# More passes of a zero tile in TensorE's planned gaps of the first stage, and a last store in two parts

## The chip, the core and the metric

One core of a Trainium2 chip runs the whole program. Its engines are TensorE (PE in the rows, with its weight loads as PEld), VectorE (DVE), ScalarE (ACT), GpSimd (POOL) and SyncE (SP, which issues all DMAs here). Each takes its instructions strictly in order, and they wait for each other by semaphores. The metric is the device time of one execution in microseconds (us).

## The reference

Causal attention over 4 x 12 heads of 448 x 64, then two feed-forward layers over 1792 tokens of 768 numbers:

```python
scores = scale * np.matmul(q, k.transpose(0, 1, 3, 2))     # causal mask, softmax
x = np.matmul(attn, v)                                     # -> (1792, 768)
h = (x @ w1) * (x @ w2) @ w3
x = h @ w_out                                              # d_ff 1024
h = x @ w_in                                               # d_ff 2048
out = (h - np.tanh(h)) @ w_out2
```

## The kernel before

The product w3 times w_out does not depend on the tokens. The kernel forms it first, as sixteen tiles of 128 x 384, and weaves this with the attention of the first two batches: that is the first stage, up to about 150 us. Numbers are split in a high and a low part, so that each product is three matmuls on fp32r operands (L598 to L600: high times low, low times high, high times high); the products of the attention run on plain float32.

For one pair of heads the attention goes round the engines: scores on TensorE (L683), masking and row maximum on VectorE (L646), exponentials on ScalarE (L696), 20 transposes of the probabilities on TensorE (L720), their copies `pt` out of PSUM on ScalarE (L341), probabilities times values on TensorE (L749) with four transposes of the reciprocal sums (L759), a copy `xp` on ScalarE (L763) and its scaling on VectorE (L765). ScalarE, VectorE and GpSimd also convert the weights that arrive by DMA (`raw`, L382 to L399; high part L341, low part L344).

The order of all instructions is set when the program is built, by a planner (`Plan`). Each piece of work is a flow that asks for an engine and a time; `run` picks what can start first, by planned times. Where TensorE's next instruction would by plan start more than `GAP` after the end of the one before it, `run` calls `plan.idle` with the planned gap. That function (in `start`) issues a number of passes of `none`, a 128 x 128 tile of zeros, into columns 384 and up of the second PSUM tile, which hold zeros and which nobody reads. The planner books no time for these passes. `plan.idle` is set for the first stage alone. Thirteen such passes (`WARM`) stand ahead of all other work of TensorE.

In the last stage (`Second.lowered`) each product of the last layer is added into an accumulator on VectorE (L1382) and, in the last quarter, stored by SP (L1389). The last product is quarter 3, pair 2, i = 6 of the second half. Behind the last store SP comes to the end of the program: a branch on a flag (L1798), which skips a second body that computes the same without an approximation, and the closing barriers.

Of the kernel before, what the change touches and what calls it, by code (L numbers as in the profile page):

```python
# [23 lines left out]
ALU = mybir.AluOpType  # L24

B, H, S, D = 4, 12, 448, 64
NT, DM, FF, FF2 = 1792, 768, 1024, 2048
P = 128
# [102 lines left out]
class Plan:  # L131


    LAG, DMA_LAG, MARGIN = 0.12, 2.0, 0.5
    FILLER, GAP = 1000, 1.0

    def __init__(self):
        self.free = dict.fromkeys(("PE", "ACT", "DVE", "POOL", "DMA"), 0.0)
# [116 lines left out]
def act(n, psum=False):  # L255
    return "ACT", (0.104 if psum else 0.147) + n / 1400
# [3 lines left out]
def dve(n):  # L260

    return "DVE", 0.068 + n / 960
# [25 lines left out]
def dma(size):  # L288
    return "DMA", max(0.5, size / 330e3)
# [3 lines left out]
def body(ctx: ExitStack, tc: tile.TileContext, qkd, vd, vd4, w12, w3t, wo, w_in, wo2, out, flag=None):  # L293
    nc = tc.nc
    V, A, G, SP, PE = nc.vector, nc.scalar, nc.gpsimd, nc.sync, nc.tensor
# [44 lines left out]
    def copy(eng, out, in_):  # L340
        A.copy(out=out, in_=in_) if eng == "ACT" else V.tensor_copy(out=out, in_=in_)  # L341
# [810 lines left out]
    class Second:  # L1152
# [218 lines left out]
        def lowered(self, q, pair, i, buf, seen):  # L1371

            out_ = {0: (0, 0), 1: (0, 0), 2: (0, 1), 3: (1, 1), 4: (1, 1), 5: (0, 1), 6: (1, 0)}[i]
            m, t = 2 * pair + out_[0], out_[1]
            a = self.acc[pair].t[:, out_[0], t * S:(t + 1) * S]
            if i in (1, 4, 5):
                yield seen[{1: 0, 4: 3, 5: 2}[i]]
            if q == 0 and i in (0, 2, 3, 6):
                copy((yield [act(S, True), dve(S)]), a, buf.t[:, :S])
            else:  # L1380
                yield dve(S)
                V.tensor_tensor(out=a, in0=buf.t[:, :S], in1=a, op=ALU.add)  # L1382
            plan.set(seen[i])
            if i in (1, 5, 6):
                plan.done(buf)
            if q == 3 and i in (1, 4, 5, 6):
                yield dma(P * S * 4)
                d = self.half * W + t * S
                SP.dma_start(out=out[m, :, d:d + S], in_=a)  # L1389
                self.left[pair] -= 1  # L1390
                if self.left[pair] == 0:
                    plan.done(self.acc[pair])
# [41 lines left out]
    def first_half(r_asb, r_raw, r_t, r_u, x):  # L1434
        yield from product(r_asb, r_raw, r_t, jobs_12, jobs_in + jobs_out, [wps[m] for m in WP] + w12s + twos)
        plan.spawn(sums(pairs_in, r_u), 500)
        plan.spawn(sums_out(pairs_out, r_u), 500)
        ab = []
        for _ in range(2):
            ab.append((yield r_g))  # L1440
        yield from bilinear(jobs_12, x.t, x_ready[:2], r_asb, ab, ab_ready[0])
        plan.done(x)
        plan.set(l1_over)
        tile = project(wps, ab, ab_ready[0], 0, lambda m: r_st[0], opened)
        for m in WP:
            yield from tile(m, range(8), there_and_back())
        for a in ab:
            plan.done(a)
        plan.set(l2_over)

    def start(r_asb, r_raw, r_t, r_u, at, aps):
        none = at.tile([P, P], F32R, name="none")
        V.memset(none.bitcast(F32), 0.0)
        V.memset(r_mm.tiles[1][:, 384:], 0.0)

        def idle(gap):

            for _ in range(int(0.7 * (gap - 0.5) / 0.107)):
                PE.matmul(r_mm.tiles[1][:, 384:], none, none, start=False, stop=False, skip_group_check=True)

        plan.idle = idle
        for _ in range(WARM):
            PE.matmul(r_mm.tiles[1][:, 384:], none, none, start=False, stop=False, skip_group_check=True)
        x = yield r_x
        xa["over"] = attention(at, aps, x.t)
        plan.spawn(first_half(r_asb, r_raw, r_t, r_u, x), plan.FILLER)
        plan.set(spawned)
# [336 lines left out]
```

## Time and profile before

| | us |
|---|---|
| median of three runs (lowest, highest) | 1010.18 (1008.81, 1011.15) |
| profiled execution, its own time | 1009.07 |
| span of its trace | 1007.3 |
| TensorE busy | 987.6 |
| VectorE busy | 796.1 |
| ScalarE busy | 624.7 |

A row of the time line gives the start, the duration, the engine and line, what is written and read, and how many instructions run together; in brackets the idle time of the engine before it and what ended that. A matmul's duration reaches to its modelled end and overlaps the next one, so the spacing of starts tells the rate. A plain float32 product of L683 or L749 has two rows in the trace. The granted clock (PEclk) is given as a share of 2.4 GHz; 0.50 is the level of 1.2 GHz.

### The profile page before, as it was taken

The page shows a single profiled execution, that of the slowest core. Times are in us where ns is not written, and L with a number is a line of the kernel's source. Part 1 is how long each engine was busy: PE and PEld are TensorE (multiplying, and loading weights), DVE is VectorE, ACT ScalarE, POOL GpSimd, SP SyncE. Part 2 cuts the span into 40 slices and gives each one's busy share as a digit, 9 for nine tenths or more (in the row PEclk, how much of TensorE's full clock was granted, in tenths as well). Part 3 has the DMA queues.
Part 4 walks back from the last instruction along what each step waited for, and adds up shares of the span by engine and source line. Part 5 has one row for each costly group of instructions (what it writes and reads, how often), then busy time and mean ns, then how long its engine had stood idle before and what let it go on. Part 6 is the DMA issues. An engine that isn't in the chain of part 4 may idle for free.

```text
span 1007.3 us, 20299 instructions
## 1 busy us (share of the span) xinstructions
PE 987.6 (98%) x7437; PEld 867.9 (86%) x7437; DVE 796.1 (79%) x1759; ACT 624.7 (62%) x1482; POOL 94.6 (9%) x76
## 2 busy tenths in 40 slices
PE   9889999999999999999999999999999999999997
PEld 6668678888888889899889899999999999999996
DVE  6778885777778657888887388897999896869894
ACT  7997775877778624444445456886676656645540
POOL 2443201122232110000000000000000000000000
PEclk9999999999999999999999999999999999999999
DMA  7566648767786789899999878978689786666443
GB/s 239 190 207 203 216 135 272 266 204 251 249 312 214 247 312 331 292 322 318 320 337 366 320 266 294 320 260 263 228 292 312 213 254 201 182 191 182 146 136 114
DMA packets 119021, 251.25 MB, mean 249 GB/s; under 512 B 11072, under 2 KB 70464, under 8 KB 118144
## 3 DMA queue, kind: packets, MB, share of 16 engines
q1 hardware_dynamic: 118912, 249.87, 73.9%
q8 instruction: 60, 0.98, 0.4%
q14 instruction: 49, 0.40, 0.1%
HBM read 170.20 MB, written 79.63 MB: 248 GB/s over the span
## 4 chain that ended last, share of the span: by engine, by line
PE 86%; ACT 5%; DVE 4%; DMA 3%; issue 1%; POOL 0%; SPq 0%; DVEq 0%; ACTq 0%
PE mm L598 13%; PE mm L600 12%; PE mm L599 12%; PE mm L1363 7%; PE mm L1188 7%; PE mm L1187 7%; PE mm L1365 7%; PE mm L1189 7%; PE mm L1364 7%; PE pv L904 3%; PE sc L884 3%; DMA raw<-w3t 1%; ACT p L696 1%; DMA raw<-wo 1%; PE att L749 1%; ACT pt L341 1%
## 5 line engine op out<-in xcount | busy, mean ns | idle before, releaser
L598 PE MATMUL mm<-x,hl 128*128 128x384 f32 (+1 forms) x384 | 141.9, 369 | 0.0
L600 PE MATMUL mm<-x,hl 128*128 128x384 f32 (+1 forms) x384 | 139.5, 363 | 0.0
L599 PE MATMUL mm<-x,hl 128*128 128x384 f32 (+1 forms) x384 | 139.4, 363 | 0.0
L1188 PE MATMUL mm<-x,hl 128*128 128x448 f32 x336 | 122.8, 365 | 0.0
L1189 PE MATMUL mm<-x,hl 128*128 128x448 f32 x336 | 122.7, 365 | 0.0
L1187 PE MATMUL mm<-x,hl 128*128 128x448 f32 x336 | 122.7, 365 | 0.0
L1382 DVE TENSOR_TENSOR acc<-mm,acc 128x448 f32<-128x448 f32 x144 | 89.2, 620 | 21.8 <-PE mm L1365 21.1
L598 PE MATMUL mm<-g,hl 128*128 128x384 f32 (+1 forms) x272 | 98.5, 362 | 2.4 <-POOL g L344 2.4
L382 ACT ACTIVATE raw<-raw 128x512 uint32<-128x512 uint32 (+1 forms) x80 | 64.1, 802 | 56.9 <-DMA raw<-w 17.2
L599 PE MATMUL mm<-g,hl 128*128 128x384 f32 (+1 forms) x272 | 95.2, 350 | 0.9 <-POOL hl L344 0.9
L600 PE MATMUL mm<-g,hl 128*128 128x384 f32 (+1 forms) x272 | 95.2, 350 | 0.0
L598 PEld LDWEIGHTS mm<-x,hl 128*128 128x128 f32 x384 | 72.0, 188 | 10.8 <-issue 2.5
L600 PEld LDWEIGHTS mm<-x,hl 128*128 128x128 f32 x384 | 72.1, 188 | 7.7
L599 PEld LDWEIGHTS mm<-x,hl 128*128 128x128 f32 x384 | 72.1, 188 | 7.4
L399 DVE CUSTOM_DVE_ANT_0 t<-raw,t 128x1024 uint16<-128x1024 uint16 (+1 forms) x80 | 69.5, 868 | 4.8 <-ACT raw L382 0.5
L395 DVE SCALAR_TENSOR_TENSOR t<-raw,t 128x512 uint32<-128x512 uint32 (+1 forms) x80 | 70.5, 881 | 1.2
L1187 PEld LDWEIGHTS mm<-x,hl 128*128 128x128 f32 x336 | 63.1, 188 | 5.2
L1188 PEld LDWEIGHTS mm<-x,hl 128*128 128x128 f32 x336 | 63.1, 188 | 5.1
L1189 PEld LDWEIGHTS mm<-x,hl 128*128 128x128 f32 x336 | 63.1, 188 | 4.9
L344 POOL TENSOR_TENSOR hl<-t,hl 128x512 fp32r<-128x512 f32 (+1 forms) x32 | 51.1, 1598 | 173.7 <-ACT hl L341 130.2
L341 ACT CAST x<-x 128x256 fp32r<-128x256 f32 (+2 forms) x83 | 39.7, 495 | 36.2 <-DMA x<-scx 17.7
L392 DVE TENSOR_SCALAR t<-raw 128x512 uint32<-128x512 uint32 (+1 forms) x80 | 44.0, 550 | 22.3 <-POOL hl L344 6.9
(190 smaller groups left out, 2346.0 us busy)
## 6 DMA issues: line engine op xcount, KB each, us to landing
scs<-hl SPq DMA_DIRECT2D x56, 384.0 KB, 4.3
hl<-scs SPq DMA_DIRECT2D x56, 384.0 KB, 3.3
raw<-w SPq DMA_DIRECT2D x16, 768.0 KB, 6.1
raw<-w_in SPq DMA_DIRECT2D x16, 768.0 KB, 6.2
raw<-wo SPq DMA_DIRECT2D x24, 512.0 KB, 5.7
sco<-cvo SPq DMA_DIRECT2D x24, 512.0 KB, 5.6
qk<-qkd SPq DMA_DIRECT2D x24, 448.0 KB, 3.9
v<-vd SPq DMA_DIRECT2D x12, 896.0 KB, 7.4
```

Source lines behind the costliest of these rows:

```text
L395: V.scalar_tensor_tensor(out=t, in0=raw[:, :n, 1], scalar=0xC0000000, in1=t, op0=ALU.bitwise_and, op1=ALU.bitwise_or)
L399: V.tensor_tensor(out=t, in0=t, in1=raw[:, :n, 0], op=ALU.add)
L598: PE.matmul(ps, wh, xl, start=k == 0, stop=False)
L599: PE.matmul(ps, wl, xh, start=False, stop=False)
L600: PE.matmul(ps, wh, xh, start=False, stop=k == last)
L1187: PE.matmul(ps, wh, xl, start=first and k == 0, stop=False, skip_group_check=True)
L1188: PE.matmul(ps, wl, xh, start=False, stop=False, skip_group_check=True)
L1189: PE.matmul(ps, wh, xh, start=False, stop=k == KH - 1, skip_group_check=True)
L1363: PE.matmul(ps, wh, xl, start=first and k == 0, stop=False, skip_group_check=True)
L1364: PE.matmul(ps, wl, xh, start=False, stop=False, skip_group_check=True)
L1365: PE.matmul(ps, wh, xh, start=False, stop=k == 1, skip_group_check=True)
L1382: V.tensor_tensor(out=a, in0=buf.t[:, :S], in1=a, op=ALU.add)
```

## The change

Two numbers and a formula of the planner, and one store. `GAP` goes from 1.0 to 0.6, so passes are also put into shorter planned gaps. Their number was 0.7 times the gap less 0.5, over 0.107; it becomes the gap less 0.25, over 0.107. In all there are 108 passes in place of 54. In `lowered` the addition and the store of the last product are cut into two halves of 224 columns.

```diff
-    FILLER, GAP = 1000, 1.0
+    FILLER, GAP = 1000, 0.6
...
+            cuts = [(0, S)]
+            if (self.half, q, pair, i) == (1, 3, 2, 6):
+                cuts = [(0, S // 2), (S // 2, S)]
             if q == 0 and i in (0, 2, 3, 6):
                 copy((yield [act(S, True), dve(S)]), a, buf.t[:, :S])
             else:
-                yield dve(S)
-                V.tensor_tensor(out=a, in0=buf.t[:, :S], in1=a, op=ALU.add)
+                for o, e in cuts:
+                    yield dve(e - o)
+                    V.tensor_tensor(out=a[:, o:e], in0=buf.t[:, o:e], in1=a[:, o:e], op=ALU.add)
...
-                yield dma(P * S * 4)
                 d = self.half * W + t * S
-                SP.dma_start(out=out[m, :, d:d + S], in_=a)
+                for o, e in cuts:
+                    yield dma(P * (e - o) * 4)
+                    SP.dma_start(out=out[m, :, d + o:d + e], in_=a[:, o:e])
...
         def idle(gap):
-            for _ in range(int(0.7 * (gap - 0.5) / 0.107)):
+            for _ in range(int((gap - 0.25) / 0.107)):
                 PE.matmul(r_mm.tiles[1][:, 384:], none, none, start=False, stop=False, skip_group_check=True)
```

The order of the other instructions stays as it was on every engine; only passes are added on TensorE. By place, in the order of time, the groups go from 16, 13, 0, 4, 3, 13, 0, 0, 5, 0 passes to 26, 21, 3, 9, 7, 21, 3, 3, 10, 5. Three of the places follow; `none` is the zero tile, `qk` queries and keys, `p` the probabilities, `g` and `hl` the parts of w_out and w3.

TensorE at the start, the first two pairs of heads:

```order
 L683 MATMUL att<-qk 112x224 x2
 L683 MATMUL att<-qk 112x112 x2
-L1459 MATMUL mm_82<-none 128x128 x16
+L1464 MATMUL mm_82<-none 128x128 x26
 L683 MATMUL att<-qk 112x336 x2
 L683 MATMUL att<-qk 112x224 x2
 L683 MATMUL att<-qk 112x112 x2
-L1459 MATMUL mm_82<-none 128x128 x13
+L1464 MATMUL mm_82<-none 128x128 x21
 L720 MATMUL att<-ident,p 112x112 x20
+L1464 MATMUL mm_82<-none 128x128 x3
 L683 MATMUL att<-qk 112x448 x2
```

Ten passes more stand ahead of the second pair's scores, eight more ahead of the first transposes, and three behind those.

TensorE at about 30 us of the trace before, ahead of a product of w3 and w_out:

```order
 L683 MATMUL att<-qk 112x224 x2
 L683 MATMUL att<-qk 112x112 x2
-L1459 MATMUL mm_82<-none 128x128 x4
+L1464 MATMUL mm_82<-none 128x128 x9
 L598 MATMUL mm_81<-g,hl 128x384
 L599 MATMUL mm_81<-g,hl 128x384
 L600 MATMUL mm_81<-g,hl 128x384
```

Five passes more stand between the scores and the product.

TensorE at about 38 us, within the transposes of the third pair:

```order
 L600 MATMUL mm_82<-g,hl 128x384
 L720 MATMUL att<-ident,p 112x112 x8
-L1459 MATMUL mm_82<-none 128x128 x3
+L1464 MATMUL mm_82<-none 128x128 x7
 L720 MATMUL att<-ident,p 112x112 x12
 L598 MATMUL mm_81<-g,hl 128x384
```

Four passes more part the first eight transposes from the other twelve.

## Rows read from the trace of the kernel before

**Rows 1.** Page, part 1: busy us (share of the span) xinstructions.

```profile
PE 987.6 (98%) x7437; PEld 867.9 (86%) x7437; DVE 796.1 (79%) x1759; ACT 624.7 (62%) x1482; POOL 94.6 (9%) x76
```

**Rows 2.** Chain of waits in order of time, 9 to 60: start us, us, what.

```profile
13.88 3.18 ACT p L696 x12
...
17.06 2.02 ACT pt L341 x3
```

**Rows 3.** Time line, TensorE, 29 to 45.

```profile
29.61 0.66 PE L1459 MATMUL mm<-none 128*128 128x128 f32 x4
32.04 0.44 PE L598 MATMUL mm<-g,hl 128*128 128x384 f32 x1 [1.77 <-POOL g L344]
...
32.76 3.41 PE L749 MATMUL att<-pt,v 112*64 112x448 f32 x16
36.09 0.93 PE L759 MATMUL att<-ident,rr 112*128 112x112 f32 x4
...
38.10 0.53 PE L1459 MATMUL mm<-none 128*128 128x128 f32 x3
38.47 1.33 PE L720 MATMUL att<-ident,p 112*112 112x112 f32 x12
...
42.29 2.11 PE L749 MATMUL att<-pt,v 112*64 112x448 f32 x16
44.33 0.60 PE L759 MATMUL att<-ident,rr 112*128 112x112 f32 x4
```

**Rows 4.** Time line, ScalarE, 30 to 48.

```profile
37.06 0.53 ACT L763 COPY xp<-att 128x448 f32<-128x448 f32 x1 [1.47 <-PE att L759]
...
39.13 2.14 ACT L341 COPY pt<-att 112x896 f32<-112x896 f32 x3
```

**Rows 5.** Stretches: us, busy us of PE, PEld, DVE, ACT, POOL; PEclk, DMA, GB/s.

```profile
9.51:33.40 23.89, 20.65 (x160) 15.57 (x160) 21.85 (x67) 23.34 (x64) 7.91 (x5) 1.00 0.64 215
33.40:36.81 3.41, 3.41 (x19) 1.94 (x15) 2.44 (x6) 2.19 (x8) 1.14 (x1) 0.50 0.53 193
36.82:1002.70 965.88, 955.22 (x7234) 844.65 (x7232) 769.05 (x1676) 596.26 (x1408) 83.87 (x57) 1.00 0.75 251
```

**Rows 6.** The end: time line, SP's waits (total, times, longest), last store's landing.

```profile
1000.02 0.62 DVE L1382 TENSOR_TENSOR acc<-mm,acc 128x448 f32<-128x448 f32 x1 [0.59 <-PE mm L1365]
...
1000.68 0.33 SPq L1389 DMA_DIRECT2D out<-acc  x1
...
SPq L1798 <- SPq L1798: 3.0, 1, 3.0
...
DMA to landing us min/median/max: 2.8/2.8/2.8
```

**Rows 7.** Time line, TensorE and its weight loads (PEld), 0 to 19.

```profile
1.24 3.04 PE L1463 MATMUL mm<-none 128*128 128x128 f32 x13 [1.24 <-DVE mm L1454]
...
9.66 2.00 PE L1459 MATMUL mm<-none 128*128 128x128 f32 x16
...
11.59 1.67 PE L683 MATMUL att<-qk 64*112 64x336 f32 x12
...
14.70 1.82 PE L720 MATMUL att<-ident,p 112*112 112x112 f32 x14
...
15.34 0.95 PEld L720 LDWEIGHTS att<-ident,p 112*112 112x112 f32 x10 [0.30 <-ACT p L696]
...
17.41 0.79 PE L720 MATMUL att<-ident,p 112*112 112x112 f32 x6 [0.89 <-DVE st L646]
...
18.13 2.15 PE L683 MATMUL att<-qk 64*112 64x448 f32 x16
```

**Rows 8.** TensorE's waits, 0 to 130: us in total, times, longest us.

```profile
PE att L720 <- DVE p L660: 1.6, 1, 1.6
...
PE att L683 <- DVE xp L765: 1.1, 1, 1.1
```

**Rows 9.** Time line, VectorE: masking and maximum of 224 columns.

```profile
9.78 0.39 DVE L646 CUSTOM_DVE_ANT_0 p<-att,mask 112x224 f32<-112x224 f32 x1 [1.04 <-PE att L683]
```

## The prediction

> **What bounds the kernel now.** I read the page first: TensorE is busy 98% of the span [rows 1], so on the whole the kernel is as long as TensorE's work. Nearly all of that lies outside the change; the edits touch the first 72 us and the last 7 us. So I read those two pieces.
>
> In the first stage (attention woven with w3 times w_out) the chain of waits does not run over TensorE. From 11 to 30 us nearly all of it is ScalarE: exponentials, then the copies pt that empty the transposes, and at its end GpSimd's subtraction [rows 2]. What TensorE does later there costs time only where ScalarE, or that subtraction, is late for it. From 32 to 37 us the chain is on TensorE: after an idle 1.77 us that GpSimd ends, three products of w3 and the L749 products run, and ScalarE waits 1.47 us for L759 [rows 3, 4]. In the stretches of the span the granted clock is 1.00 from 9.51 to 33.40, 0.50 (the 1.2 GHz level) from 33.40 to 36.81, then 1.00 again [rows 5]. The same 16 rows of L749 take 3.41 us there and 2.11 us at 42.29; the four of L759 take 0.93 and 0.60 [rows 3]. So the one low-clock stretch of the stage follows its longest idle time, and it stands where TensorE is waited for.
>
> At the end, the last addition of VectorE runs 0.62 us from 1000.02, the last store is issued at 1000.68, and it lands 2.8 us later, at 1003.5. But SP has a wait of its own of 3.0 us there, in the branch at L1798, right behind the issue [rows 6]; the issue ends at 1001.01, so the branch holds SP until about 1004. The landing lies within it.
>
> **The change part by part.**
>
> *The price of a pass.* The 16 passes from 9.66 take 2.00 us [rows 7], of which the last one is about 0.28: (2.00 - 0.28)/15, 0.115 us each. The planner books no time for them, so nothing else moves in the order; whatever they last beyond the real gap is delay of the next real instruction.
>
> *First three groups, 16 to 26, 13 to 21 and a new 3.* Behind the passes of before the score products start at 11.59 and the transposes at 14.70 without idle time [rows 7]: the passes already fill the real gaps. The 10 + 8 more put the transposes back by up to 18 x 0.115 = 2.07 us. Of this 0.30 us is wait for ScalarE in mid-group, so TensorE would stand about 1.8 us late. The first eight transposes are ready at about 14.70 + 0.30 + 8 x 0.11 = 15.9 us (14 take 1.82 with that wait), and ScalarE takes them at 17.06 [rows 2, 7], which covers 1.1 to 1.2 us. So ScalarE, and with it the chain, is 0.6 us late. The later half of the transposes, at 17.41, had 0.89 us of idle and is late by what VectorE is; the 3 passes ahead of 18.13 add 0.35 to that, some 0.85 together, and the chain by then runs on ScalarE, 0.6 late. Term: +0.6. Bounds: 0 if the cover is larger than I count (TensorE's earlier instructions have slack that the waits don't show), 2.07 + 0.35 = 2.4 if nothing covers.
>
> *4 to 9 at 29.61.* Five more are 0.58 us in an idle time of 1.77 us that ends with GpSimd's result, not with TensorE [rows 3]. Covered: 0. What is late next is still that result.
>
> *3 to 7 at 38.10.* The transposes follow at 38.47 without idle, and ScalarE's copies of them start at 39.13 and run on without a gap, so the second copy soon needs them [rows 3, 4]. 4 x 0.115 = 0.46 us with little cover: +0.4, between 0 and 0.46.
>
> *The other groups.* 13 to 21 at about 45 is 8 x 0.115 = 0.92 us in the 1.1 us for which L683 waits for VectorE's xp [rows 8]. The 3, 3 and 5 new ones and the 5 to 10 at 61 are 3 or 5 passes more, 0.35 to 0.58 us each, in a stretch whose chain is ScalarE's, and TensorE meets later waits for other engines that take them up. I take 0; the upper bound is 3 + 3 + 5 + 5 passes, 1.8 us.
>
> *The clock.* With the five more passes the idle time at 30 shrinks from 1.77 us to about 1.2 (TensorE and GpSimd both come some 0.6 later there, which leaves the difference as it is). If the clock stays up, L749 and L759 take 2.11 and 0.60 us as at 42.29, in place of 3.41 and 0.93: 1.6 us less on TensorE, of which ScalarE can use the 1.47 us that it waits [rows 3, 4]. Term: -1.5, or 0 if the clock falls all the same. I take -1.5, as waits of 1.1 and even of 1.6 us (L720, for VectorE's p) later in the stage did not bring it down: from 36.82 to the end of the work it is 1.00 [rows 5, 8].
> The Trainium skill ("TensorE: Matmul & The Clock Gate", section "Why this matters for your kernels") warns only of idle gaps longer than any in this stage; by it the clock would not have fallen at 33.4 and the passes had nothing to win. Here the trace disagrees, since it fell behind an idle 1.77 us; what the rule would give is the first rival's time.
>
> *The last store.* VectorE's addition becomes two halves. No row has this addition at 224 columns; the nearest, L646, which reads the same kind of source, takes 0.39 us there [rows 9], so two halves take 0.78 in place of 0.62 and the second ends 0.16 us later. The first store's issue, 0.33 us [rows 6], ends before that. SP reaches its branch 0.16 us later, at most 0.33 (if the two issues stand in a row). A gain would need the landing to be last; it isn't, by 0.5 us. Term: +0.15, between 0 and 0.33.
>
> **The sum.** +0.6 + 0.4 - 1.5 + 0.15 = -0.35, say -0.4 us. The profiled execution took 1009.07 us (span 1007.3, 1.8 around it), 1.1 less than the median of the three runs, which range from 1008.81 to 1011.15. They differ by steps about as large as one low-clock stretch costs, so I set the sum against the mean of all four, 1009.8: **1009.4 us**.
>
> **The rivals.**
>
> *The clock falls all the same* (there, or a little later). For it: 1.2 us of idle time are left, and the passes are added work at every other place. Against: the wait of 1.6 us that left the clock alone [rows 8]. +0.6 + 0.4 + 0.15 = +1.15: 1010.9 us.
>
> *Passes ahead of the rise of the clock* (the slower side). At the start the 13 warm-up passes take 3.04 us, 3.04/13 = 0.23 us or a little less each, against 0.115 from 9.66 on [rows 7]: the clock rose only just ahead of the first group. Where it rises after it, ten more passes there cost up to 2.2 us in place of 1.15, and the 16 of before have already eaten the 1.1 us of cover: 2.2 + 8 x 0.115 - 0.30 = 2.8, with 0.4 and 0.15 it is +3.35, or +1.85 if the later fall is avoided: 1011.7 to 1013.2 us. It decides from the point where the clock rises later than about 9.7. The one trace can't say how often.
> The Trainium skill (same page, section "Part 1: The HAM clock gate") says that the point of the rise differs from run to run of one kernel, since the monitor is not started with it; by it this rival is to be reckoned with, and no run here shows it.
>
> *The delays are covered* and the clock stays up. For it: ScalarE and VectorE are busy nearly all the time from 9.51 to 33.40 [rows 5], so TensorE may have more slack than single waits show. -1.5 + 0.15: 1008.4 us; with a second low-clock stretch gone that the longer runs may have had, 1006.9.
>
> *The change does nothing*: the passes fill planned gaps, and where these aren't gaps on the chip they are only delay. That is within the first rival.
>
> **How the numbers follow.** My forecast 0.45, the fall all the same 0.25, the covered delays 0.20, the late rise 0.10. About 0.2% (2 us) is what a measurement of this kernel can tell from no change. Faster than that: the lower half of the covered case and the edge of the forecast, 0.15; slower: the late rise and the edge of the first rival, 0.12; within: 0.73. The range leaves out the late rise and the lower half of the covered case: from 1008.4 down by the spread of runs to 1007.6, and from 1010.9 up to 1011.5. The upper ends of the terms together, 2.4 + 0.46 + 1.8 + 0.33 - 1.5 = +3.5 us, would need that no cover holds anywhere; the range goes half that far.
>
> **What would show it.** Right: no stretch with a granted clock of 0.50 between 10 and 100 us; L749 at 32 to 35 us in 2.1 us; the transposes at 14.7 start 1.5 to 2 us later and ScalarE's first copy pt at 17.5; the w3 products at 32.04 at 32.6; the second half of the last addition ends 0.1 to 0.2 us later after the last product, and SP's branch still takes 3.0. Wrong: a low-clock stretch anywhere in the first 130 us, the first copy at 17.0 (covered) or beyond 18.5 (late rise or no cover), or a branch so short that the landing is last.

## The result, and the profile after

The changed kernel took 1017.93 us in the median of 7 runs (1013.43 to 1023.23), the kernel before 1008.81 (1008.56 to 1011.15). The ratio is 1.0082, with an interval of 1.0054 to 1.011: about 0.8% slower, and outside the range that I gave. The profiled execution took 1014.38 us; its span is 1012.6 against 1007.3, so 5.3 us of the loss can be read in the traces.

**The first stage shows no loss of this size.** Stretches of the span (columns as in [rows 5]):

```profile
10.00:32.00 22.00, 20.93 (x173) 17.23 (x172) 20.14 (x58) 20.21 (x52) 6.78 (x5) 1.00 0.58 198
32.00:37.00 5.00, 3.79 (x27) 2.52 (x28) 4.73 (x13) 5.00 (x16) 1.29 (x2) 1.00 0.58 174
37.00:100.00 63.00, 58.93 (x422) 47.68 (x421) 49.35 (x134) 55.25 (x144) 26.74 (x19) 1.00 0.63 210
```

The stretch at 0.50 of [rows 5] is gone. The time line of TensorE, 9 to 41 us, answers to [rows 3, 7] (L1464 are the passes):

```profile
9.48 3.12 PE L1464 MATMUL mm<-none 128*128 128x128 f32 x26
12.53 1.40 PE L683 MATMUL att<-qk 64*112 64x336 f32 x12
13.86 2.56 PE L1464 MATMUL mm<-none 128*128 128x128 f32 x21
16.25 1.52 PE L720 MATMUL att<-ident,p 112*112 112x112 f32 x14
18.68 0.79 PE L720 MATMUL att<-ident,p 112*112 112x112 f32 x6 [0.91 <-DVE st L646]
...
30.76 1.22 PE L1464 MATMUL mm<-none 128*128 128x128 f32 x9
33.21 0.44 PE L598 MATMUL mm<-g,hl 128*128 128x384 f32 x1 [1.23 <-POOL g L344]
...
33.93 2.11 PE L749 MATMUL att<-pt,v 112*64 112x448 f32 x16
35.97 0.60 PE L759 MATMUL att<-ident,rr 112*128 112x112 f32 x4
...
40.79 1.57 PE L683 MATMUL att<-qk 64*112 64x448 f32 x8
```

TensorE is 1.55 us late at the transposes (16.25 against 14.70) and 1.17 us late at the w3 product (33.21 against 32.04). L749 then takes 2.11 in place of 3.41 us, and the scores at 40.79 start at the same time in both traces. In these two traces the passes had won about what they had cost; at 341 us the changed kernel stands only 0.19 us behind (341.03 against 340.84, below).

**The loss lies at 341 to 362 us**, in the second stage, 270 us behind the last edited place ahead of it. TensorE's waits from 150 us to the end of its work; before's trace has no row there:

```profile
PE pv L904 <- issue: 3.2, 3, 2.3
```

"issue" is time in which TensorE waited for nothing that the profile shows. L904 is the product of turned probabilities and values: bursts of 96 or 104 matmuls on 32 partitions, some 14 ns each, between runs of wide matmuls (L598 to L600, about 0.2 us each). TensorE's time line, after:

```profile
341.03 0.90 PE L904 MATMUL pv<-pt,v 32*64 32x128 f32 x45
342.60 0.90 PE L904 MATMUL pv<-pt,v 32*64 32x96 f32 x51 [0.66 <-issue]
...
348.28 0.82 PE L904 MATMUL pv<-pt,v 32*64 32x64 f32 x56
349.34 0.86 PE L904 MATMUL pv<-pt,v 32*64 32x32 f32 x48 [0.24 <-issue]
...
351.72 1.21 PE L904 MATMUL pv<-pt,v 32*64 32x128 f32 x73
355.21 0.56 PE L904 MATMUL pv<-pt,v 32*64 32x96 f32 x23 [2.28 <-issue]
```

and the same three bursts before, each in one piece:

```profile
340.84 1.52 PE L904 MATMUL pv<-pt,v 32*64 32x128 f32 x96
...
347.14 1.44 PE L904 MATMUL pv<-pt,v 32*64 32x64 f32 x104
...
350.11 1.52 PE L904 MATMUL pv<-pt,v 32*64 32x128 f32 x96
```

Count the matmuls between the waits. From the first wait to the second TensorE runs 51 small, 21 wide and 56 small matmuls: 128. From the second to the third it runs 48, 6 and 73: 127. Each matmul comes with a weight load, so that is 256 instructions (other instructions, such as semaphore events, make up the odd one). The profile's queues name what comes in such pieces, before and after:

```profile
q8 instruction: 60, 0.98, 0.4%
...
q8 instruction: 61, 1.00, 0.4%
```

After, that is 61 packets of together 1.00 MB, 16 KB each, in a queue of the kind "instruction"; before it is 60. 7491 pairs of a load and a matmul, at 128 to a packet, make 58.5. So the kernel fetches TensorE's instructions in packets of 16 KB, 128 matmuls each, and all three waits stand where such a block ends. The change put 54 passes, 108 instructions, ahead of all of the second stage. Every block end of that stage so moved by 54 matmuls, from the wide matmuls behind the bursts into the bursts.

The Trainium skill ("Runtime: NRT & Kernel Launch", section "Instruction fetch mechanics") gives the size, 16 KiB and 256 instructions, and the trace agrees with its 128 pairs. It also says that the cost of passing such a boundary is mostly hidden; here it showed, with 0.24 to 2.28 us.

**The sum of the profiled execution.** Behind before, in us: 0.19 at 341.03; 4.13 behind the third wait (355.69 against 351.56 at the next wide matmul), so 3.94 for three waits with their restarts; 4.59 at the last addition (1004.61 against 1000.02), where a fourth, shorter interruption at 361 adds most of the 0.46; and 0.70 in the closing, which makes the 5.3.

The end (last additions, and SP's waits in the last ten us, answering to [rows 6]):

```profile
1004.61 0.69 DVE L1386 TENSOR_TENSOR acc<-mm,acc 128x224 f32<-128x224 f32 x2 [0.59 <-PE mm L1365]
...
SPq L1803 <- SPq L1803: 4.8, 3, 2.8
```

Two halves take 0.69 us where the whole took 0.62. The branch on the flag (now L1803) still takes 2.8, but behind it SP waits another 2 us on itself, where before's rows have 3.0 in all.

### The profile page after: what moved, and what is told of

Its sections match the earlier page's. It is cut to its first block, busy times and chain, and to the rows that moved or that the text cites. A ratio compares the mean times of both kernels' runs of the same rounds, so it can differ in the third digit from the quotient of the medians.

```text
span 1012.6 us, 20410 instructions
## 1 busy us (share of the span) xinstructions
PE 992.2 (98%) x7491; PEld 873.5 (86%) x7491; DVE 795.5 (79%) x1760; ACT 623.3 (62%) x1482; POOL 93.8 (9%) x76
## 4 chain that ended last, share of the span: by engine, by line
## 5 line engine op out<-in xcount | busy, mean ns | idle before, releaser
L598 PE MATMUL mm<-x,hl 128*128 128x384 f32 (+1 forms) x384 | 141.9, 369 | 0.0
L600 PE MATMUL mm<-x,hl 128*128 128x384 f32 (+1 forms) x384 | 139.5, 363 | 0.0
L1386 DVE TENSOR_TENSOR acc<-mm,acc 128x448 f32<-128x448 f32 (+1 forms) x145 | 88.9, 614 | 19.3 <-PE mm L1365 18.8
L598 PE MATMUL mm<-g,hl 128*128 128x384 f32 (+1 forms) x272 | 98.6, 362 | 1.9 <-POOL g L344 1.9
L600 PE MATMUL mm<-g,hl 128*128 128x384 f32 (+1 forms) x272 | 95.3, 350 | 0.0
L598 PEld LDWEIGHTS mm<-x,hl 128*128 128x128 f32 x384 | 72.0, 188 | 10.7 <-issue 2.5
L600 PEld LDWEIGHTS mm<-x,hl 128*128 128x128 f32 x384 | 72.1, 188 | 7.7
L344 POOL TENSOR_TENSOR hl<-t,hl 128x512 fp32r<-128x512 f32 (+1 forms) x32 | 51.1, 1600 | 174.7 <-ACT hl L341 130.8
L344 DVE TENSOR_TENSOR x<-x 128x256 fp32r<-128x256 f32 (+2 forms) x90 | 46.7, 530 | 22.7 <-ACT x L341 22.2
```

What stands on the lines that cost most here:

```text
L344: (V if eng == "DVE" else G).tensor_tensor(out=out, in0=in0, in1=in1, op=ALU.subtract)
L598: PE.matmul(ps, wh, xl, start=k == 0, stop=False)
L600: PE.matmul(ps, wh, xh, start=False, stop=k == last)
L1386: V.tensor_tensor(out=a[:, o:e], in0=buf.t[:, o:e], in1=a[:, o:e], op=ALU.add)
```

## The experiments

Theory: the loss is no work of the change but the place of TensorE's code. Rivals: the work of the passes, the store, or the mere length of the code.

**The passes alone, and the store alone.** The first is before with the two edits to `GAP` and the number of passes, the second before with only the last addition and store in two parts.

```diff
-    FILLER, GAP = 1000, 1.0
+    FILLER, GAP = 1000, 0.6
-            for _ in range(int(0.7 * (gap - 0.5) / 0.107)):
+            for _ in range(int((gap - 0.25) / 0.107)):
```

> The passes of the change alone, the last store in one piece as before. Theory (code): TensorE's instructions come in blocks of 16 KB by DMA; 54 passes more are 108 instructions more, so the ends of the blocks fall elsewhere in the bursts of L904, and TensorE waits there for code. Then this is like the changed kernel: 3 to 10 us above the kernel before, idle time of L904 that ends with nothing visible (issue) of 2 to 8 us. Rival (store): the loss comes with the two halves of the store, and this is within 1 us of the kernel before.

> The last store in two halves alone, passes as before. Theory (code): TensorE's instructions are those of the kernel before, so no new waits of L904; the end is 0.15 us later: 1008.8 to 1009.2 us. Rival (store): 1012 us or more.

Passes alone: 1015.06 us, ratio 1.0059 (1.0039 to 1.0078), and TensorE's waits behind 150 us are nearly those of the whole change:

```profile
PE pv L904 <- issue: 3.7, 3, 2.3
```

Store alone: 1009.48 us, ratio 1.0006 (0.9985 to 1.0027), and no such row. The passes make the loss.

**Their work, or their place in the code.** The 54 passes that the change adds are shrunk to 32 x 32, so that they do a small part of the work but are as many instructions:

```diff
+            for _ in range(int((gap - 0.25) / 0.107) - n):
+                PE.matmul(r_mm.tiles[1][:32, 384:416], none[:, :32], none[:, :32], start=False, stop=False, skip_group_check=True)
```

> The full passes of the kernel before, and each of the 54 added passes shrunk to 32 x 32: as many instructions as the changed kernel, little of the added work. Theory (code): the ends of the code blocks are where the changed kernel has them, so TensorE waits for code in L904 as there: 1012 to 1020 us, issue waits of 2 us or more in the profile. Rival (time): the loss comes from the work and the shift in time of the full passes; with a third of that work 1009 to 1010 us and no issue waits.

1016.05 us, ratio 1.0062 (1.0043 to 1.0082), "PE pv L904 <- issue" 3.3 us in three waits. The loss doesn't come from the work of the passes; their number makes it.

**More code, with the block ends back in place.** All passes of the change in full, and 74 small ones more (37 ahead of the w3 product at 32 us, 37 ahead of the first transposes of the seventh pair): 54 + 74 = 128, one whole block. Once with one last store, once with the changed kernel's two.

```diff
+            calls[0] += 1
+            for _ in range(37 if calls[0] == 4 else 0):
+                PE.matmul(r_mm.tiles[1][:32, 384:416], none[:, :32], none[:, :32], start=False, stop=False, skip_group_check=True)
...
+                if n == 6 and js == (0,):
+                    plan.small(37)
```

> The passes of the changed kernel (store in one piece) and 74 small passes of 32 x 32 more, half of them ahead of the w3 product at 32 us and half ahead of the transposes of the seventh pair at 96 us, where TensorE idles: 128 matmuls with their weight loads more than the kernel before, that is 256 instructions or one block of 16 KB at 64 bytes each. Theory (code): from 97 us on the ends of the blocks stand to the bursts of L904 as in the kernel before, and the waits for code go away: 1007.5 to 1009.5 us. Rival (time): the full passes are all there and so is the loss, 1013 us or more. Rival (more code costs more): above the changed kernel.

> The changed kernel, store in two parts and all, with 74 small passes (37 ahead of the w3 product at 32 us, 37 ahead of the first transposes of the seventh pair), so that 128 matmuls more than before's stand ahead of the later code and the block ends fall where they did. Theory: no issue wait at L904, ratio 0.998 to 1.003 to before. Rival (the store in two parts and the passes together cost what neither showed alone): ratio above 1.004 without issue waits.

One store: 1009.7 us, ratio 1.0007 (0.9989 to 1.0025). Two stores: 1009.58 us, ratio 1.0009 (0.999 to 1.0028). Neither has an issue wait, and the bursts run in one piece (time line of TensorE, the kernel with two stores):

```profile
339.60 1.52 PE L906 MATMUL pv<-pt,v 32*64 32x128 f32 x96
...
345.90 1.44 PE L906 MATMUL pv<-pt,v 32*64 32x64 f32 x104
...
348.87 1.52 PE L906 MATMUL pv<-pt,v 32*64 32x128 f32 x96
```

So the change with 148 instructions on top is as fast as before. The three rivals (work, store, length of the code) fall.

**Other places.** 27 and 91 small passes added to before.

```diff
+            for _ in range({3: 27}.get(calls[0], 0)):
...
+            for _ in range({2: 17, 3: 37}.get(calls[0], 0)):
```

> The kernel before with 27 small passes (32x32) added behind the group of 4 at 30 us: 54 more instructions, which move the ends of TensorE's code blocks 27 matmuls earlier in the work behind. Theory: the ends at 337 to 361 us fall on the 72nd of the 96 small matmuls, the 83rd of the 104, and four matmuls behind the third burst; from the stalls of the changed kernel (0.7, 0.2 and 2.3 us at the 45th, 56th and 73rd) and the time that a block takes here, issue waits of 0.5 to 1.4 us at the first, 0 to 0.3 at the second, and 0.8 to 1.2 at the third, which now stands at L598 to L600: 1.5 to 2.9 us in all, and 0.3 to 1.5 us over the kernel before if the clock stretch goes with them. Rival (only a shift of about half a block hurts, or the stalls have no place in the code): no issue wait.

> The kernel before with 91 small passes added (17 at 15 us, 37 at 31 us, 37 ahead of the first transposes of the seventh pair): block ends 91 matmuls earlier. Theory: they fall on the 8th, 19th and 36th matmul of the same three bursts; a block then holds the bursts with few wide matmuls between, its 128 matmuls run in 3.3 to 4.4 us, and the next block is there no sooner than some 5.4 to 5.9 us behind the last: issue waits of 3 to 4.5 us in all, 1.5 to 3.5 us slower than before. Rival (more instructions cost in proportion): between the result of 54 more and twice that, 7 to 9 us slower. Rival (it matters only where an end lies past the middle of a burst): under 1 us of issue waits.

With 27: 1011.25 us, ratio 1.0024 (1.0009 to 1.0038). The ends stand where they were expected, on the 72nd and the 83rd small matmul and on the fourth wide one behind the third burst, with 2.0 us of waits, within the forecast. The time is not: 2.5 us above the 1008.76 us of before's runs beside it, where 0.3 to 1.5 was expected. The stretch at 0.50 didn't go; its trace has two of them in the first stage, from 45.67 and from 96.87. The waits (time line of TensorE):

```profile
341.94 0.56 PE L904 MATMUL pv<-pt,v 32*64 32x96 f32 x24 [0.21 <-issue]
...
348.68 0.55 PE L904 MATMUL pv<-pt,v 32*64 32x32 f32 x21 [0.29 <-issue]
...
354.87 0.50 PE L599 MATMUL mm<-x,hl 128*128 128x512 f32 x1 [1.46 <-issue]
```

With 91 the forecast failed: 1008.42 us, ratio 1.0009 (0.9993 to 1.0026), and no wait at all, although the ends lie inside the bursts. An end inside a burst is not enough. I had taken the time from one block's end to the next block's arrival as fixed, 5.4 to 5.9 us; it isn't. The last rival (only an end past the middle of a burst matters) fits this number, but not its neighbours: the changed kernel waits at an end on the 45th of 96, and the next experiment runs through an end on the 73rd of 96 without a wait.

**What the fetch waits for.** The changed kernel's passes, but of the twelve 1 MB loads of stored product weights only an eighth is loaded.

```diff
+                    if ring is r_hl and a.users == 1 and a.n == 1024:
+                        SP.dma_start(out=a.buf.t[:, :, :128].bitcast(F32), in_=x[:, :, :128])
+                        continue
```

> The passes of the changed kernel with one last store, and of the twelve 1 MB loads of stored product weights (L549, hl<-scp) only an eighth of the columns is loaded, so the later columns hold what was there before. The 336 to 362 us stretch then moves about a third less. Theory A (TensorE uses up a block of code faster than the next can come, loads or not; the fetches took 0.95 us with the queues full and 0.88 to 0.96 with them empty): issue waits at L904 as before, 2.5 to 3.7 us. Theory B (the fetches start late because data transfers stand ahead of them): issue waits under half, below 1.5 us.

1009.38 us, ratio 1.0015 (1.0002 to 1.0028): of 3.7 us of waits 0.2 is left, and the third burst, which held the 2.3 us, runs in one piece (time line of TensorE):

```profile
346.17 0.86 PE L907 MATMUL pv<-pt,v 32*64 32x32 f32 x48 [0.24 <-issue]
...
348.54 1.58 PE L907 MATMUL pv<-pt,v 32*64 32x128 f32 x96
```

The block ends stand where they stood with the waits. Theory A falls, B holds. The stretches from the passing of a block end to the start of the next packet of the instruction queue show it (columns as in [rows 5]; the last two are DMA share and GB/s). After:

```profile
337.24:340.33 3.09, 3.09 (x92) 2.67 (x85) 2.36 (x8) 2.40 (x9) 1.12 (x1) 1.00 0.87 351
342.60:347.04 4.44, 4.44 (x67) 3.79 (x68) 0.18 (x1) 2.47 (x8) 0.00 (x0) 1.00 0.93 305
349.34:352.71 3.37, 3.37 (x126) 2.79 (x127) 3.27 (x5) 0.59 (x2) 0.00 (x0) 1.00 0.93 327
```

With the light loads, at the same three ends:

```profile
335.01:335.66 0.65, 0.65 (x72) 0.65 (x66) 0.50 (x3) 0.28 (x2) 0.65 (x1) 1.00 0.00 0
339.44:343.94 4.50, 4.50 (x83) 3.83 (x76) 0.68 (x5) 2.55 (x8) 0.00 (x0) 1.00 0.86 287
346.17:347.27 1.10, 1.10 (x49) 1.04 (x50) 0.70 (x2) 0.21 (x1) 0.00 (x0) 1.00 0.17 60
```

Where the DMA engines are idle, the packet starts 0.65 and 1.10 us after the end was passed; where they are busy with loads and stores, 3 to 4.5 us after. In ten traces, at all block ends from 330 to 362 us: 10 with a DMA share under 0.3 in that time waited 0.17 to 1.7 us, and of 40 with a share over 0.6, 36 waited 2.3 to 4.6 us. From there the packet takes mostly 0.88 to 1.05 us, and at the four interruptions of after's trace TensorE goes on 1.31 to 1.47 us behind its end. These times come from the records of the single packets and from counting instructions:

| block passed at | packet starts, after us | landed, after us | next end reached, after us | next block begun, after us |
|---|---|---|---|---|
| before, 337.62 | 2.50 | 3.46 | 5.13 | 5.31 |
| before, 342.93 | 3.72 | 4.69 | 6.62 | 6.85 |
| before, 349.78 | 2.50 | 3.45 | 6.42 | 6.43 |
| after, 337.24 | 3.09 | 4.05 | 4.45 | 5.36 |
| after, 342.60 | 4.44 | 5.39 | 6.28 | 6.74 |
| after, 349.34 | 3.37 | 4.42 | 3.37 | 5.87 |
| 91 more, 344.20 | 0.45 | 1.40 | 3.29 | 3.29 |
| light loads, 346.17 | 1.10 | 1.98 | 3.36 | 3.39 |

A wait appears where a block is run through sooner than the next packet has landed plus about 1.4 us. In after's third block the 127 matmuls are nearly all small and gone in 3.37 us, while the packet only starts. The kernel with 91 more has a block as short (3.29 us), but there the packet started after 0.45 us. Why it did so with the engines busy, as in the three other cases that don't fit, I did not settle. The same trace shows more: one packet started at 330.43, 3.1 us before the block end at 333.52 was passed, and the next one only at 341.03, 3.2 us behind the end at 337.88, which TensorE passed without a wait. There the code was fetched earlier than the table's pattern has it, so how far ahead the fetch runs isn't fixed either. And before was near the edge itself: 5.13 against 3.46 + 1.4 leaves some 0.3 us.

**The changed kernel once more.**

> The changed kernel once more, for a second trace of it. Theory (TensorE's blocks of code, 128 matmuls each, end inside the bursts at L904 while the fetch of the next one stands behind loads): issue waits at L904 again, on the 45th, 56th and 73rd matmul of the same three bursts, 2.5 to 4 us in all, and 1013 to 1020 us. If the waits are of the same size while the time is again 8 us longer than before's, most of the difference outside the waits has another cause.

1017.88 us, ratio 1.009 (1.0056 to 1.0124). TensorE's waits in this second trace, from 150 us on:

```profile
PE pv L904 <- issue: 3.7, 3, 2.5
```

and the stretches around the longest of them (columns as in [rows 5]):

```profile
340.00:354.50 14.50, 10.84 (x306) 8.69 (x291) 7.28 (x16) 5.16 (x16) 0.00 (x0) 1.00 0.91 305
354.56:357.97 3.41, 3.41 (x21) 2.55 (x11) 0.00 (x0) 0.00 (x0) 0.00 (x0) 0.50 0.85 344
358.00:372.00 14.00, 14.00 (x170) 12.78 (x169) 4.37 (x6) 4.28 (x8) 2.47 (x2) 1.00 0.50 172
```

Behind the wait of 2.5 us the granted clock fell to 0.50 for 3.41 us, in the trace of the small passes too (355.7 to 359.2), not in after's first trace. TensorE was 3.13 us behind before's trace at the restart, 4.64 at 357.9: the fall costs 1.5 us on top. So a profiled execution of 1014.4 and a median of 1017.9 can go together. But this execution took 1014.5 us as well, since its first stage was 1 to 2 us earlier.

What the 3 us more of most runs are, no trace of the changed kernel shows. The mean granted clock that each run has on record points at such falls: it is 0.995 over the eleven runs of the changed kernel and 0.998 over the twenty of the two kernels with the ends back in place. Over 1014 us that makes some 6 us more at 0.50, or 1.7 stretches of 3.41 us; at 1.5 us each they would cost some 2.5 us (an estimate). The longest run, 1023.23 us at 0.996, doesn't fit this. And the one trace of a long execution, that of the small passes (1017.61 us), has a loss of another kind: from about 800 us to the end its matmuls start every 206.7 ns, in before's trace every 202.7, both at a granted clock of 1.00 and without waits. That is nearly all of the 4.1 us that it loses to before's trace behind 700 us; its cause is open.

**The clock term by itself.** Before with its 54 passes dealt out otherwise, so that no code behind them moves:

```diff
+        counts = [14, 13, 9, 2, 11, 5]
-            for _ in range(int(0.7 * (gap - 0.5) / 0.107)):
+            for _ in range(counts.pop(0)):
```

> The kernel before with the same 54 passes and the same number of TensorE instructions, five passes moved into the gap after the w3 product's predecessor: groups of 16, 13, 4, 3, 13, 5 become 14, 13, 9, 2, 11, 5; one last store. Theory (the 54 more passes did their work in the first stage and lost it through the place of the later code): no stretch at 0.50 between 10 and 100 us, no issue wait at L904, 1.0 to 1.8 us faster than before (ratio 0.9982 to 0.9990), near the limit of what five rounds tell. Rival (the cleared clock stretch is no gain, as both kernels of the case stand level at 40.79 us): ratio 0.9995 to 1.0005.

1008.09 us, ratio 1.0002 (0.9991 to 1.0014): nothing won, since the clock fell all the same. TensorE's time line:

```profile
31.52 0.44 PE L598 MATMUL mm<-g,hl 128*128 128x384 f32 x1 [1.23 <-POOL g L344]
...
32.24 3.80 PE L749 MATMUL att<-pt,v 112*64 112x448 f32 x16
```

and the stretch with its clock (columns as in [rows 5]):

```profile
32.39:35.79 3.40, 3.40 (x16) 1.51 (x14) 2.90 (x6) 2.67 (x8) 0.65 (x1) 0.50 0.43 144
```

The idle time is the 1.23 us of after's trace, where the clock stayed up. So the idle time at that place doesn't decide it, and moving five passes there is not enough. The added passes as a whole do go with a clock that stays up: in all seven traces of kernels that have them, full or small, no stretch at 0.50 lies between 10 and 100 us, although with the small ones TensorE idles 1.63 us at that place. All five traces without them have one or two, starting at 32 to 33.4 us in three of them and at 45 us or later in the two with 27 and 91 small passes more. Which of the added passes do it is not shown. No kernel of the study was faster than before.

## Why the prediction was wrong

**The step that failed** is the second sentence of the prediction's reading: "Nearly all of that lies outside the change; the edits touch the first 72 us and the last 7 us. So I read those two pieces." With it goes "The planner books no time for them, so nothing else moves in the order", the ground on which a pass was priced at 0.115 us of TensorE's time and nothing else. The order indeed stayed. But 108 instructions more ahead of a later stage move the ends of that stage's code blocks, and this cost 4 to 6 us at 341 to 362 us in the four traces that have such waits in full, some ten times the size of my sum of -0.4, and with the other sign. No term, and none of the rivals, was about it; the slower rival (passes ahead of the clock's rise) was another mechanism at another place. The right page of the profile was at hand: 60 packets in the instruction queue, and bursts of a hundred matmuls in 1.5 us, with the DMA engines 0.93 to 0.99 busy behind the block ends there.

**The first stage's delays: +0.6, in after's trace 1.2 to 1.6 us at 16 to 33 us.** I let ScalarE's lateness set the term, with 1.1 to 1.2 us of cover. ScalarE's first copies indeed came only 0.18 us later (17.24 against 17.06). But the second part of the transposes waits for VectorE (18.68 against 17.41), and VectorE was late for two reasons. Its time line with GpSimd's (POOL), after:

```profile
13.40 0.51 DVE L646 CUSTOM_DVE_ANT_0 p<-att,mask 112x336 f32<-112x336 f32 x1 [0.41 <-PE att L683]
13.83 1.59 DVE L392 TENSOR_SCALAR t<-raw 128x768 uint32<-128x768 uint32 x1
...
13.73 1.28 POOL L344 TENSOR_TENSOR hl<-t,hl 128x512 fp32r<-128x512 f32 x1 [11.42 <-ACT hl L341]
```

and before:

```profile
13.09 0.50 DVE L646 CUSTOM_DVE_ANT_0 p<-att,mask 112x336 f32<-112x336 f32 x1
13.52 0.56 DVE L392 TENSOR_SCALAR t<-raw 128x768 uint32<-128x768 uint32 x1
...
13.97 1.28 POOL L344 TENSOR_TENSOR hl<-t,hl 128x512 fp32r<-128x512 f32 x1 [11.67 <-ACT hl L341]
```

First, VectorE now waits for the score products between the two groups of passes, which ten more passes had put back by 0.94 us (12.53 against 11.59); that alone makes it 0.31 us late (13.40 against 13.09). Second, its conversion of weights at L392 takes 1.59 us in place of 0.56, and that is most of the delay. In after's trace it starts while GpSimd's L344 runs, in before's ahead of it. The trace of the passes alone has the same (1.60 us, started within L344); in the ten other traces, the second one of the changed kernel among them, it takes 0.55 or 0.56. That the two engines hold each other up is read from these two traces and not tested. So the 1.2 to 1.6 us are in the main a meeting that the added passes don't always bring about, and they don't measure my +0.6. The w3 product came at 33.21 in after's trace and at 31.09 in the second one, not at 32.6.

**3 to 7 at 38.10: +0.4**, and the others at 0: not separable. From the w3 product on, the two traces close up, and by 40.79 they are level. Nor does one pair of traces tell the sum of the stage. At the matmul that stands at 160 us in before's trace, after is 0.47 us behind, the second trace of the changed kernel 0.90 us ahead, and the trace of the store alone, whose first stage is before's, 1.62 us behind. The spread is larger than the sum that I forecast.

**The clock: -1.5.** In after's trace it came as written, 1.30 us at L749 and 0.33 at L759, and no trace with all the added passes has a stretch at 0.50 in the first stage. But my reason, the idle time shortened from 1.77 to 1.2 us, is not the one: with five passes moved there the idle time was 1.23 us and the clock fell.

**The store: +0.15, between 0 and 0.33.** Too small. From the end of the last product to SP's branch it is 1.07 us in eight traces with one store and 1.31 or 1.32 in four with two; from there to the end of the span 5.92 to 6.44 (mean 6.08) against 6.29 to 6.66 (mean 6.55). Together that is about 0.7 us. I had said that the branch hides the landing by 0.5 us. The last half now lands 3.2 to 3.3 us after the branch begins, in before's trace 2.4, so just behind the branch's end; and the second wait behind the branch is longer. The timed runs can't resolve it: 1.0006 alone.

**Passes ahead of the clock's rise** didn't occur in after's trace (the clock is up from 9.04, the passes start at 9.48). The rise stands between 6.4 and 9.5 us in the twelve traces, at 9.04 and 6.40 in the two of the changed kernel, so the Trainium skill's remark that it differs from run to run ("TensorE: Matmul & The Clock Gate", section "Part 1: The HAM clock gate") is shown here.

## What to carry to other kernels

An instruction on a full engine costs its time and its place: whatever adds instructions ahead of dense bursts of small matmuls moves where code blocks end, and a later stage can lose more than the edit wins. When a loss stands far from the edit, look for waits on "issue", count the instructions between them, and put in a filler that makes the shift a whole block (here 128 matmuls); if the loss goes, it was the place. And a term of half a microsecond can't be checked on one pair of traces where a stage's end moves by 1 to 2 us from one execution to the next.

## What the runs showed of the hardware that I had not expected

- A wait for code: TensorE stood 0.2 to 2.6 us at ends of 128-matmul blocks where it ran a block in 3.4 to 6.3 us and the DMA engines were 0.81 to 0.98 busy until the next packet started. With the loads lightened the largest of the waits was gone.
- Instruction packets start late where data transfers fill the engines: a packet of 16 KB started 0.17 to 1.7 us after the end of the block before with idle DMA engines, mostly 2.3 to 4.6 us with busy ones.
- A wait of 2.0 to 2.6 us for code was followed by a granted clock of 0.50 for 3.41 us in two traces, and not in two others; idle times of 1.23 us at 31 us were followed by it in one kernel and not in another.
- TensorE's rate can fall without its granted clock: with the small passes the matmuls of the last layer started every 206.7 ns in place of 202.7 from about 800 us on, at a granted clock of 1.00.
